# Attention over channels, then a squared-relu feed-forward: w_out combinations in one go on DVE, fold blocks in the output banks, the first group's output fourteen tiles behind

## The chip, the cores and the metric

One core of one Trainium2 chip. The metric is the device time of one execution in microseconds (us), lower is better. Engines are named as in the profile: PE (TensorE matmul), PEld (its weight loads), DVE (VectorE), ACT (ScalarE), POOL (GpSimd), SP (SyncE).

## The reference, cut to what matters

```python
# q, k, v: (4, 6080, 256) float32; w_in 256 x 2048, w_out 2048 x 256
qn = q / (norm(q, axis=1) + 1e-6);  kn = k / (norm(k, axis=1) + 1e-6)
a  = softmax(kn.T @ qn / tau)                 # 256 x 256, one for each batch
x  = (v @ a).reshape(24320, 256)
h  = x @ w_in
out = (s * relu(h)**2 + b) @ w_out
```

## The kernel before

Four ideas have to be known. (1) The attention matrix is folded into w_in: for each batch `wa = a @ w_in`, so v is multiplied by `wa` directly. (2) Tokens go in 48 groups of 512. A group has 16 *steps*, one for each tile of 128 of the 2048 hidden columns; PE does two matmuls of 512 columns a step (`mm1`), ACT a relu for each two steps. (3) All groups but the first and the last form the second product with seven instead of eight block products (`seven_items`), which needs combinations T1, T2, T3, N4 of the blocks of w_out; they are made once, during groups 0 and 1. (4) Side work is put at given steps by `at_step`, and what stands before it on an engine counts.

```python
def bank(self, name, a, b):                       # PSUM for one-off work of a batch
    if self.b == 0 and name != "wa_ps":
        return ps_o.tile(...)                     # pool of three output banks
    return ps_gram.tile(...)                      # the single Gram bank
...
def fold_one(f0, n, m):                           # a block of wa: 512 columns, one half m
    def f():
        wa_ps = self.bank("wa_ps", CH, C)...
        fold_mm(f0, n, m, wa_ps)                  # two matmuls of 512
        scaled(f0, n, m, wa_ps)                   # m == 0: evicted by ACT; m == 1: by DVE
...
def rowconst_sum(i):                              # rowconst = b * column sums of w_out
    if i < NPIECE - 1: acc = (w_pieces[0] or acc) + w_pieces[i + 1]      # DVE, 128x1024 f32
    else:              fold acc to a half                                # DVE
def rowconst_mm():
    rc_ps = ps_gram.tile(...)                     # again the Gram bank
    matmul(rc_ps, ones32, acc[:, 0, :]); rowconst = rc_ps * b            # DVE
def combine_w(i, step):                           # piece i of w_out, blocks B11 B12 B21 B22
    if step == 0:
        T1 = B12 - B11; B12 = B22 - B12           # DVE
        T3 = copy(B12)                            # ACT
    else:
        B12 = B12 + B11                           # DVE: must wait for T3's copy
        T2 = copy(B12)                            # ACT
        N4 = B21 - B12                            # DVE
...
for i, f in enumerate(fin[7:]): at_step(i // 2 * 4 + i % 2 + 1, f)       # six fold blocks
for i in range(NPIECE + 1):     at_step(14 + 2 * i, rowconst_sum(i))
at_step(26, rowconst_mm)
for i in range(NPIECE):
    for step in range(2):       at_step(24 + 2 * i + step, combine_w(i, step))
...
PLAG = {0: 12, NG - 1: 5}       # plain output of group 0 runs 12 steps behind mm1
for s in range(NS + FT):
    g, m = divmod(s, FT)
    mm1(g, m)
    ...seven-product items of group g - 1, from m == 3 on; plain output steps...
    if m % 2 == 1: relu(g, m // 2)                # ACT; frees one of two h banks
    ...squares and S sums (DVE, ACT)...
    for f in side.pop(s, []): f()
```

The Gram matmuls of batch 1 (the first product of attention, `kn.T @ qn`, in `ps_gram`) begin at step 26. An *h bank* is the PSUM memory that mm1 writes and the relu reads; there are two. S1, S2 and so on are the sums of g (the squared relu) that the seven products need. The copy that turns group 1's tokens into `vT` (eight transposes on PE, one copy on DVE) stands at step 12.

## Time and profile before

| | before |
|---|---|
| median of 3 runs, then of 4 | 747.0, then 745.96 us |
| span in the profile | 745.0 us |
| PE, DVE, ACT busy | 95%, 84%, 72% |
| PE busy between 200 and 400 us | 198.54 of 200 us |

The table says: PE bounds the kernel except at its beginning. The prediction shows the lines; in the timeline a line gives start, duration, engine, source line, operation, tiles written and read, count, and in brackets how long the engine was idle before and what ended it.

### The profile page before, as it was taken

The numbers are of one execution on the slowest core, as the hardware profiler recorded it, in microseconds if no ns is written. First come the engines' busy times: TensorE is split into PE (matmuls) and PEld (weight loads), VectorE is DVE, ScalarE is ACT, GpSimd is POOL, SyncE is SP. The second block draws the span as 40 slices with busy tenths as digits, with TensorE's granted clock in tenths as the row PEclk, the third lists the DMA queues.
The fourth block names the chain that finished last, engine by engine and source line by source line (L and its number), as shares of the span: only waits on it lengthen the run. The fifth ranks groups of instructions, "written<-read, shape, count | busy, mean of one in ns | idle before, by whom it ended". The sixth has DMA issues, their size and how long they took to land.

```text
span 745.0 us, 17832 instructions
## 1 busy us (share of the span) xinstructions
PE 711.1 (95%) x7614; PEld 511.6 (69%) x7614; DVE 626.4 (84%) x872; ACT 538.1 (72%) x573; POOL 83.7 (11%) x159
## 2 busy tenths in 40 slices
PE   4777999999999999999999999999999999999997
PEld 3534677776677777777668777777767777777776
DVE  4757799988888899989779898988888888888886
ACT  5456777777877777777777877877787777777872
POOL 5522211000102002000200111000000000000000
PEclk9999899999999999999999999999999999999999
DMA  9999959324645686432564646623332333321201
GB/s 236 209 254 133 206 116 149 70 67 102 133 90 108 123 140 119 96 91 66 110 132 114 130 98 126 136 65 72 83 71 63 72 97 73 92 61 44 79 29 73
DMA packets 83664, 80.61 MB, mean 108 GB/s; under 512 B 55712, under 2 KB 58592, under 8 KB 83584
## 3 DMA queue, kind: packets, MB, share of 16 engines
q0 software_dynamic: 23536, 40.51, 31.8%
q1 hardware_dynamic: 59616, 37.64, 19.1%
q8 instruction: 60, 0.98, 0.6%
q10 hardware_dynamic: 432, 1.31, 0.5%
q14 instruction: 20, 0.16, 0.1%
HBM read 81.00 MB, written 24.90 MB: 142 GB/s over the span
## 4 chain that ended last, share of the span: by engine, by line
PE 82%; DVE 6%; ACT 5%; DMA 4%; issue 2%; POOL 0%; DVEq 0%; ACTq 0%; POOLq 0%
PE h_ps L535 40%; PE o_ps L677 35%; PE s_ps L142 4%; ACT r L545 2%; DVE g L558 2%; DMA qk<-in_q_dram 2%; DMA qk<-in_k_dram 1%; PE wa_ps L274 1%; DMA w_in<-in_moe_w_in_dram 1%; ACT g L556 1%; DVE wa L269 1%; PE o_ps L583 1%; DVE S L603 1%; ACT wa L267 1%; DVE o_sb L563 1%
## 5 line engine op out<-in xcount | busy, mean ns | idle before, releaser
L545 ACT ACTIVATE r<-h_ps 128x1024 f16<-128x1024 f32 (+1 forms) x384 | 387.8, 1013 | 167.4 <-PE h_ps L535 165.2
L535 PE MATMUL h_ps<-vT,wa 128*128 128x512 f16 (+7 forms) x1632 | 454.6, 366 | 7.0 <-ACT r L545 5.7
L677 PEld LDWEIGHTS <-S 128*128 128x128 f16 x2944 | 198.3, 98 | 85.8 <-DVE S L603 1.0
L677 PEld LDWEIGHTS <-g 128*128 128x128 f16 x2208 | 155.9, 98 | 76.3 <-issue 2.6
L558 DVE TENSOR_TENSOR g<-r 128x2048 f16<-128x2048 f16 (+2 forms) x154 | 176.8, 1149 | 24.9 <-ACT r L545 24.8
L677 PE MATMUL o_ps<-T,S 128*128 128x128 f16 x2208 | 183.5, 219 | 1.0 <-DVE S L603 0.7
L535 PEld LDWEIGHTS <-wa 128*128 128x128 f16 x1632 | 136.6, 98 | 29.9 <-issue 7.4
L677 PE MATMUL o_ps<-w_out,g 128*128 128x128 f16 x1472 | 135.1, 220 | 0.0
L563 DVE SCALAR_TENSOR_TENSOR o_sb<-o_ps,s_out,u 128x256 f32<-128x256 f32 x138 | 66.5, 482 | 57.7 <-PE o_ps L677 54.3
L556 ACT ACTIVATE g<-r 128x1024 f16<-128x1024 f16 x92 | 96.7, 1051 | 0.0
L319 POOL DMA_DIRECT2D v<-in_v_dram x48 | 25.7, 537 | 536.1 <-DMA vT<-v 354.1
L142 PE MATMUL s_ps<-qk 128*128 128x256 f16 (+1 forms) x384 | 70.1, 283 | 15.6 <-ACT qk L133 6.8
L563 DVE SCALAR_TENSOR_TENSOR u<-o_ps,s_out,rowconst 128x256 f32<-128x256 f32 x138 | 65.9, 477 | 2.6 <-PE o_ps L677 2.6
L677 PE MATMUL o_ps<-N,g 128*128 128x128 f16 x736 | 63.4, 219 | 0.9 <-ACT nrm L222 0.9
L677 PE MATMUL o_ps<-w_out,S 128*128 128x128 f16 x736 | 63.4, 219 | 0.0
L165 ACT ACTIVATE sq<-qk 128x1024 f16<-128x1024 f16 (+3 forms) x49 | 50.5, 1034 | 11.4 <-DMA qk<-in_k_dram 7.4
L605 DVE TENSOR_TENSOR S<-S,g 128x2048 f16<-128x2048 f16 x46 | 56.3, 1224 | 1.3
L607 DVE TENSOR_TENSOR S<-g 128x2048 f16<-128x2048 f16 x46 | 55.9, 1215 | 0.0
L603 DVE TENSOR_TENSOR S<-g 128x2048 f16<-128x2048 f16 x46 | 55.9, 1215 | 0.0
L609 DVE TENSOR_TENSOR S<-g,S 128x2048 f16<-128x2048 f16 x46 | 55.9, 1214 | 0.0
L142 PEld LDWEIGHTS <-qk 128*128 128x128 f16 (+1 forms) x384 | 32.8, 101 | 21.2 <-issue 8.9
L162 DVE TENSOR_TENSOR sq<-qk 128x1024 f16<-128x1024 f16 (+3 forms) x49 | 33.0, 673 | 2.2 <-DMA qk<-in_q_dram 2.1
(67 smaller groups left out, 279.3 us busy)
## 6 DMA issues: line engine op xcount, KB each, us to landing
out_dram<-o_sb SPq DMA_DIRECT2D x46, 512.0 KB, 3.0
v<-in_v_dram POOLq DMA_DIRECT2D x47, 256.0 KB, 3.8
qk<-in_k_dram POOLq DMA_DIRECT2D x42, 256.0 KB, 6.6
qk<-in_q_dram POOLq DMA_DIRECT2D x42, 256.0 KB, 7.4
vT<-v SPq DMA_TRANSPOSE x182, 2.8
w<-in_moe_w_out_dram POOLq DMA_DIRECT2D x4, 512.0 KB, 13.6
raw<-in_q_dram ACTq DMA_DIRECT2D x2, 512.0 KB, 6.6
raw<-in_k_dram SPq DMA_DIRECT2D x2, 512.0 KB, 6.4
```

The source lines that it names most:

```text
L142: po(nc.tensor.matmul(self.s_ps[:, ch, :], kc[:np_, j, ts(ch, P)], qc[:np_, j, :], start=(c == 0 and j == 0 and ch == 0), stop=(c == len(s ...
L165: po(nc.scalar.activation(out=st["sq"][:np_, 1, js, :], in_=kc[:np_, js, :], func=AF.Square))
L535: po(nc.tensor.matmul(dst, wa[:, ci, ts(m, P)], src, start=(ci == 0), stop=(ci == CH - 1), skip_group_check=True))
L545: po(nc.scalar.activation(out=r16[:, :, i % 2, :n], in_=h_tiles.pop((g, i))[:, :, :n], func=AF.Relu))
L556: po(nc.scalar.activation(out=dst, in_=src, func=AF.Square))
L558: po(nc.vector.tensor_mul(dst, src, src))
L563: po(nc.vector.scalar_tensor_tensor(out=dst, in0=src, scalar=s_out, op0=ALU.mult, in1=add, op1=ALU.add))
L603: po(nc.vector.tensor_add(S[1], A21, A22))
L605: po(nc.vector.tensor_sub(S[2], S[1], A11))
L607: po(nc.vector.tensor_sub(S[3], A11, A21))
L609: po(nc.vector.tensor_sub(S[4], A12, S[2]))
L677: po(nc.tensor.matmul(st[name][:, j, :], a()[:, i, ts(j, P)], w[:, i, :], start=first, stop=last, skip_group_check=True))
```

## The change

The intent: DVE makes a piece's four combinations without waiting for ACT (the sum goes into B11, so B12 need not be copied first), and ACT copies them five steps later; all this starts eight steps sooner. The fold blocks rotate through three output banks, so the second no longer waits for the first one's eviction; to leave these banks free, the plain output of group 0 is put two steps later. The constant row moves from steps 14 to 26 to steps 11 to 23.

```diff
         def bank(self, name, a, b):
-            if self.b == 0 and name != "wa_ps":
+            if self.b == 0:
                 return ps_o.tile([P, a, b], FP32, tag="o_ps", name=name)
...
-    def combine_w(i, step):
+    def combine_w(i):
         part = ts(i, 2)
-        if step == 0:
-            po(nc.vector.tensor_sub(T1[:, part, :], B12, B11))
-            po(nc.vector.tensor_sub(B12, B22, B12))
-            po(nc.scalar.copy(out=T3[:, part, :], in_=B12))
-        else:
-            po(nc.vector.tensor_add(B12, B12, B11))
-            po(nc.scalar.copy(out=T2[:, part, :], in_=B12))
-            po(nc.vector.tensor_sub(N4[:, part, :], B21, B12))
+        po(nc.vector.tensor_sub(T1[:, part, :], B12, B11))
+        po(nc.vector.tensor_sub(B12, B22, B12))
+        po(nc.vector.tensor_add(B11, B11, B12))
+        po(nc.vector.tensor_sub(N4[:, part, :], B21, B11))
+
+    def cast_w(i):
+        po(nc.scalar.copy(out=T2[:, ts(i, 2), :], in_=w[:, 0, :, :P]))
+        po(nc.scalar.copy(out=T3[:, ts(i, 2), :], in_=w[:, 0, :, P:]))
...
     for i in range(NPIECE + 1):
-        at_step(14 + 2 * i, lambda i=i: rowconst_sum(i))
-    at_step(26, rowconst_mm)
+        at_step(11 + i, lambda i=i: rowconst_sum(i))
+    at_step(23, rowconst_mm)
     for i in range(NPIECE):
-        for step in range(2):
-            at_step(24 + 2 * i + step, lambda i=i, step=step: combine_w(i, step))
+        at_step(16 + 2 * i, lambda i=i: combine_w(i))
+        at_step(21 + 2 * i, lambda i=i: cast_w(i))
...
-    PLAG = {0: 12, NG - 1: 5}
+    PLAG = {0: 14, NG - 1: 5}
```

More of the change, by code (lines that the diff above doesn't have):

```diff
@@ L441, in combine_w @@
         part = ts(i, 2)
-        if step == 0:
-            po(nc.vector.tensor_sub(T1[:, part, :], B12, B11))
-            po(nc.vector.tensor_sub(B12, B22, B12))
-            po(nc.scalar.copy(out=T3[:, part, :], in_=B12))
-        else:
-            po(nc.vector.tensor_add(B12, B12, B11))
-            po(nc.scalar.copy(out=T2[:, part, :], in_=B12))
-            po(nc.vector.tensor_sub(N4[:, part, :], B21, B12))
+        po(nc.vector.tensor_sub(T1[:, part, :], B12, B11))
[3 more added lines that the diff above has]
+    def cast_w(i):
+        w = w_pieces[i].rearrange("p (i h) c -> p h i c", h=2)
+        po(nc.scalar.copy(out=T2[:, ts(i, 2), :], in_=w[:, 0, :, :P]))
+        po(nc.scalar.copy(out=T3[:, ts(i, 2), :], in_=w[:, 0, :, P:]))
     side = {}
```

## The prediction

> **What bounds the kernel now.** I read the page first (busy shares and slices), then the stretches table to see where TensorE is idle, then the timeline of 39 to 83 us, where this change acts, and the DMA issues.
>
> ```profile
> PE 711.1 (95%) x7614; PEld 511.6 (69%) x7614; DVE 626.4 (84%) x872; ACT 538.1 (72%) x573; POOL 83.7 (11%) x159
> ...
> PE   4777999999999999999999999999999999999997
> ...
> PEclk9999899999999999999999999999999999999999
> ```
>
> One slice is 18.6 us. From the fifth slice on TensorE is busy throughout, at full clock but for that slice. Slices 2 to 4 (19 to 75 us) are the only weak ones after the load. The stretches table (length, PE busy, PEld, DVE, ACT, POOL, granted clock, DMA share, GB/s) says it sharply:
>
> ```profile
> 71.00:74.00 3.00, 0.00 (x0) 0.00 (x0) 2.46 (x6) 1.28 (x3) 1.07 (x2) 1.00 1.03 115
> ...
> 76.50:78.20 1.70, 1.63 (x4) 0.55 (x4) 1.70 (x4) 1.24 (x3) 1.09 (x3) 0.50 1.05 189
> 78.20:80.00 1.80, 1.80 (x12) 1.33 (x11) 1.78 (x3) 1.53 (x2) 1.04 (x2) 0.50 1.15 206
> ...
> 81.00:82.00 1.00, 1.00 (x6) 0.44 (x5) 0.58 (x2) 0.00 (x0) 0.00 (x0) 0.50 1.15 208
> ...
> 200.00:400.00 200.00, 198.54 (x2184) 143.70 (x2184) 174.89 (x239) 152.03 (x161) 20.66 (x39) 1.00 0.53 108
> ```
>
> The steady part is bound by TensorE (198.5 of 200 us). Whatever is won before 83 us therefore reaches the end nearly whole, and nothing later can be won. One step of the program is one feed-forward tile of 128; steps 0 to 15 are group 0, and the seven-product output of group 1 begins with step 35.
>
> Three waits stand in that stretch. First, the fold blocks (a pair in each four steps, all in one bank):
>
> ```profile
> 41.77 0.68 ACT L267 ACTIVATE wa<-wa_ps,rs 128x512 f16<-128x512 f32 x1
> 41.90 0.69 DVE L558 TENSOR_TENSOR g<-r 128x1024 f16<-128x1024 f16 x1 [1.73 <-ACT r L545]
> 42.50 0.59 PE L274 MATMUL wa_ps<-w_in,eT 128*128 128x512 f16 x2 [0.83 <-ACT wa L267]
> 43.13 0.75 DVE L269 TENSOR_SCALAR wa<-wa_ps,rs 128x512 f16<-128x512 f32 x1 [0.53 <-PE wa_ps L274]
> 43.94 0.82 PE L535 MATMUL h_ps<-vT,wa 128*128 128x512 f16 x3 [0.20 <-DVE wa L269]
> ```
>
> The second block's matmuls wait for ACT to empty the bank, and the next tile waits for DVE's eviction of that block. The pattern returns at 47.89 and 51.84: a period of 3.95 us, three times.
>
> Second and third, the combinations and the constant row:
>
> ```profile
> 66.96 0.48 DVE L435 TENSOR_SCALAR rowconst<-rc_ps,b_bc 128x256 f32<-128x256 f32 x1
> 67.50 0.38 PE L142 MATMUL s_ps<-qk 128*128 128x256 f16 x2 [1.69 <-DVE rowconst L435]
> 72.72 0.40 ACT L445 CAST T<-w 128x256 f16<-128x256 f32 x1 [1.99 <-DVE w L444]
> 73.16 0.43 DVE L447 TENSOR_TENSOR w<-w 128x256 f32<-128x256 f32 x1 [0.47 <-ACT T L445]
> 74.10 0.59 PE L535 MATMUL h_ps<-vT,wa 128*128 128x512 f16 x2 [3.20 <-ACT r L545]
> 76.57 1.86 PE L535 MATMUL h_ps<-vT,wa 128*128 128x512 f16 x4 [1.23 <-ACT r L545]
> ```
>
> The Gram matmul waits 1.69 us for the bank that rowconst holds behind combinations. Then DVE and ACT wait for each other's half of a combination. A relu queued behind an ACT copy is late, TensorE is without an h bank for 3.20 and 1.23 us, and its clock falls to a half (four matmuls of 512 in 1.86 us at 76.57, against 1.02 us for four at 39.79).
>
> [...] a gap of 3.2 us, clock 0.50 from 76.5 to 82. [...] the relu at 73.03 runs only after the copy of 72.72, which itself waited 1.99 us. [...] the trace has 0.42 us for 128x256, so the combinations stay as dear as they were.
>
> **The change, part by part.**
>
> (1) Combinations. Before: 4 pieces of 4 DVE operations at 0.42 us (0.46 from start to start) and 2 ACT copies at 0.40. After: the same counts, at the same durations. Work removed: none. Removed is the return: DVE no longer waits for T3's copy before overwriting B12, because the sum goes into B11; and the copies come five steps later. They also start at step 16 instead of 24, into steps where DVE had slack (before: 8.86 busy of 13.20 us in 52 to 65.2).
>
> (2) Fold blocks in three output banks. Per pair, take 40.65 as the first block's start. Its ACT eviction is unchanged (41.77). The second block's matmuls now follow tile 2 at 41.52 instead of 42.50. DVE however takes the square first, which waits for the relu: 41.90 to 42.51. Its eviction then ends at about 43.3, so tile 4 goes on at 43.32 instead of 43.94. Gain 0.62 per pair, 1.9 us in three, not the 0.98 that TensorE's own wait suggests. Step 12 is reached at about 49.2 and its second half at 50.0 instead of 51.84.
>
> (3) The constant row is summed from step 11 instead of 14. Here a new wait comes in. The pieces of w_out are loaded by these:
>
> ```profile
> w<-in_moe_w_out_dram POOLq DMA_DIRECT2D x4, 512.0 KB, 13.6
> ```
>
> They are issued at 35.70, 36.94, 40.97 and 46.35 us; asked issue by issue, they take 14.9, 14.9, 12.3 and 8.3 us, so they land at 50.6, 51.8, 53.3 and 54.7. Before, the first sum began at 55.34, just after. Now DVE reaches it at about 50.9 and stands until 51.8, and the second until 53.3 (1.21 us each). The copy of vT for group 1 is behind the second sum: 54.5 to 55.2. Step 16 needs it, so its matmul begins at about 55.2; before it was 55.66. The fold gain shrinks to 0.46 us here.
>
> (4) Lag 14. By step 16 two output steps are done instead of four, so 2 x 0.43 us of TensorE work is pushed on to steps 28 and 29. Steps 16 to 26 go at 0.87 us each as before (2 x 0.217 for mm1, 4 x 0.11 for the output): step 26 at about 63.9 instead of 64.34. DVE meanwhile, from 55.2: two squares at 0.61, the third sum 1.15, two folds at 0.58, to about 58.85; 16 combination operations at 0.455, to 66.1; rowconst to 66.6. So the Gram matmul of step 26, ready at 64.8, still waits, to 66.65 instead of 67.50. ACT's copies find their inputs ready within 0.2 us by this reckoning.
>
> (5) Steps 27 to 35: relu, last copy, relu, Gram square, relu on ACT at 0.92, 0.80, 0.92, 0.96, 0.92; TensorE fills with output steps 28 and 29 and is held by the relu of the last tile until about 72.4. The first of the seven products begins at 73.2 instead of 78.2: 5.0 us. S1 is some 0.5 us late for the second product (it follows the last square and a Gram fold on DVE): -0.5 us. The half clock from 78.2 to 82.1, 3.9 us long, cost half of that[...]: +1.9 us.
>
> Sum: 5.0 - 0.5 + 1.9 = 6.4 us. 747.0 - 6.4 = 740.6.
>
> **Rivals.** (a) All idle time goes. From 39.8 to 78.2 TensorE has 35 steps of mm1 at 0.433 (15.2), 6 blocks (2.6), 16 output steps (6.9), transposes, rc and Gram (2.6): 27.3 of 38.4 us. With the 1.9 us of clock the ceiling is 13 us, or 734. Against it: ACT and DVE each have about 27 us of work in the same steps, and dependencies leave gaps. (b) The landing of w_out eats the whole fold gain and DVE, 3 to 4 us later than planned, is the new bound up to step 35: then only the ping-pong goes (3.2 + 1.2 us of gaps, a part of the clock), 3 to 4 us, 743.5. For it: DVE's list in (4) has no slack. (c) The gap at step 26 plus a wait for a relu behind a copy still drops the clock: 1.9 us less gain, 742.5. Against it: the folding stage before, with gaps of 0.8 us in each 4 us, ran at 1.00. (d) The gain is hidden: against it stands the 198.5 of 200 us later. (e) Slower: the Gram of batch 1 or the loads behind the copies come too late; but its first chunk needs no piece's buffer, and the copies free theirs earlier than before.
>
> **Range and chances.** The sum's weakest terms are the DVE list (about 1.5 us either way) and the clock (1.9 us). Rival (a) in part gives 737, (b) with an unlucky clock 744. The runs before scatter by 2.4 us themselves. 2% is 15 us, above even the ceiling of 13: faster 0.01, within 2% 0.98, slower 0.01.
>
> **What would show it.** In the profile after: TensorE's wait for ACT wa gone from the fold blocks, and a period near 3.3 us; DVE idle on the DMA of w before the first two sums, and TensorE waiting for vT's copy around 55; no ACT copy waiting over 0.5 us for a combination; a Gram wait of about 1.8 us on rowconst near 66; the first product near 73, at full clock. Wrong: a clock of 0.50 in 70 to 80 us, waits of 3 us for relu, a first product after 76 us, or a steady part no longer at 99%.

The sum came to 5.0 - 0.5 + 1.9 = 6.4 us, so 740.6 us. The 1.9 us are half of the 3.9 us at clock 0.50 in the profile before; that they would be won whole was the estimate.

## The result, and the profile after

The changed kernel took 739.89 us (median of 4 runs, 739.74 to 740.27), the kernel before 745.96 (4 runs, 744.75 to 747.14). The ratio is 0.992, 95% interval 0.9898 to 0.9941. Here and below a ratio is the mean time of one kernel's fast runs over that of the other's fast runs of the same rounds, so not quite the ratio of the medians quoted. All runs of this case count as fast.

The page of the changed kernel, busy shares and granted clock by slice:

```profile
PE 709.0 (96%) x7614; PEld 510.3 (69%) x7614; DVE 625.7 (85%) x872; ACT 538.1 (73%) x573; POOL 83.3 (11%) x159
...
PEclk9999999999999999999999999999999999999999
```

The work is the same, with the same counts; the slice of lower clock is gone. The stretches table of the changed kernel:

```profile
71.00:74.00 3.00, 2.63 (x21) 1.47 (x19) 2.33 (x4) 2.80 (x4) 0.89 (x2) 1.00 1.12 185
...
78.00:83.00 5.00, 5.00 (x55) 3.54 (x54) 4.67 (x7) 3.33 (x4) 0.00 (x0) 1.00 1.13 206
...
200.00:400.00 200.00, 198.53 (x2207) 144.78 (x2204) 175.16 (x240) 150.62 (x158) 22.26 (x42) 1.00 0.51 107
```

Between 71 and 74 us, where PE stood still before, it is busy for 2.63 of 3 us; between 78 and 83 us the clock is 1.00, where it was 0.50 up to 82; and the steady part is as before. The timeline of the changed kernel, at the places that the prediction named:

```profile
43.56 0.82 PE L536 MATMUL h_ps<-vT,wa 128*128 128x512 f16 x3 [0.42 <-DVE wa L269]
44.22 0.59 PE L274 MATMUL wa_ps<-w_in,eT 128*128 128x512 f16 x2
...
47.55 0.59 PE L274 MATMUL wa_ps<-w_in,eT 128*128 128x512 f16 x2
...
52.90 1.23 DVE L427 TENSOR_TENSOR acc<-w,w 128x1024 f32<-128x1024 f32 x1 [1.68 <-DMA w<-in_moe_w_out_dram]
55.41 0.68 DVE L332 COPY vT<-vT_ps 128x1024 f16<-128x1024 f16 x1
56.15 0.59 PE L536 MATMUL h_ps<-vT,wa 128*128 128x512 f16 x2 [1.55 <-DVE vT L332]
...
66.26 0.48 DVE L435 TENSOR_SCALAR rowconst<-rc_ps,b_bc 128x256 f32<-128x256 f32 x1
66.79 0.38 PE L142 MATMUL s_ps<-qk 128*128 128x256 f16 x2 [0.50 <-DVE rowconst L435]
...
73.39 0.55 PE L678 MATMUL o_ps<-w_out,g 128*128 128x128 f16 x7
```

Two fold pairs begin 3.33 us apart (44.22 and 47.55) and ACT is no longer in the bracket. DVE waits 1.68 us for a piece of w_out, and PE 1.55 us for the copy of vT that stands behind it on DVE. The first of the seven products is at 73.39 us, 4.8 us sooner than the 78.2 of before, and at full clock. (The first tile of group 0 starts 0.24 us later in this trace, at 40.03 instead of 39.79 us, before anything that was changed.) What is won reaches the end: the sum S4 of group 1 starts at 81.45 us, in the kernel before at 88.10 (second fence):

```profile
81.45 1.22 DVE L610 TENSOR_TENSOR S<-g,S 128x2048 f16<-128x2048 f16 x1
```

```profile
88.10 1.21 DVE L609 TENSOR_TENSOR S<-g,S 128x2048 f16<-128x2048 f16 x1
```

That is 6.65 us, all but 0.15 of the 6.8 us between the two spans. The chain of waits of the changed kernel (start, duration, what) says what paces it from 54 to 67 us:

```profile
41.04 13.13 DMA w<-in_moe_w_out_dram
...
54.27 1.23 DVE acc L427
```

In the stretch 48 to 80 us it runs from the landing of the third piece of w_out through DVE's list to rowconst, and only then on to PE.

### The profile page after: what moved, and what is told of

Read it like the earlier page. It is cut to its first block, busy times and chain, and to the rows that moved or that the text cites. A ratio compares the mean times of both kernels' runs of the same rounds, so it can differ in the third digit from the quotient of the medians.

```text
span 738.2 us, 17834 instructions
## 1 busy us (share of the span) xinstructions
PE 709.0 (96%) x7614; PEld 510.3 (69%) x7614; DVE 625.7 (85%) x872; ACT 538.1 (73%) x573; POOL 83.3 (11%) x159
## 4 chain that ended last, share of the span: by engine, by line
PE 80%; DVE 7%; DMA 6%; ACT 4%; issue 1%; POOL 1%; DVEq 0%; POOLq 0%
PE h_ps L536 39%; PE o_ps L678 36%; PE s_ps L142 4%; ACT r L546 2%; DMA qk<-in_q_dram 2%; DMA w<-in_moe_w_out_dram 2%; DVE g L559 2%; DMA w_in<-in_moe_w_in_dram 1%; DMA qk<-in_k_dram 1%; PE wa_ps L274 1%; DVE S L604 1%; ACT g L557 1%; PE o_ps L584 1%; DVE wa L269 1%; ACT L222 1%
## 5 line engine op out<-in xcount | busy, mean ns | idle before, releaser
L142 PE MATMUL s_ps<-qk 128*128 128x256 f16 (+1 forms) x384 | 70.3, 284 | 14.2 <-ACT qk L133 7.1
```

The costliest lines, as they stand in the source:

```text
L142: po(nc.tensor.matmul(self.s_ps[:, ch, :], kc[:np_, j, ts(ch, P)], qc[:np_, j, :], start=(c == 0 and j == 0 and ch == 0), stop=(c == len(s ...
```

## The experiments

Twelve runs, each with 4 to 6 timed executions, four kernels to a chip. The kernels built on the one before scatter by some 2 us, b_filler apart (why is the first question below); those built on the changed one by 0.2 to 1.6 us (most under 1), so their medians are compared, also where two ran on different chips. Times in us:

| run | what | median | ratio to before |
|---|---|---|---|
| (the changed kernel) | | 739.89 | 0.9920 |
| b_again | before, unchanged | 745.39 | 1.0003 |
| b_filler | before + idle matmuls in the gaps | 744.84 | 0.9989 |
| b_folds | before + fold blocks in the output banks | 743.87 | 0.9976 |
| b_form | before + one-go combination, old place | 744.31 | 0.9978 |
| b_form5 | the same, copies five steps later | 743.08 | 0.9972 |
| a_oldform | changed, old combination at the new place | 742.07 | 0.9953 |
| a_onebank | changed, fold blocks in one bank | 740.50 | 0.9931 |
| a_lag12 | changed, output twelve tiles behind | 738.72 | 0.9906 |
| a_sums13 | changed, row sums from step 13 | 739.28 | 0.9917 |
| a_rc22 | the same, rowconst matmul at step 22 | 737.79 | 0.9894 |
| a_best | the same, output twelve tiles behind | 738.02 | 0.9897 |
| a_best_fold0 | the same, fold blocks at steps 0, 4, 8 | 737.00 | 0.9883 |

My theory: waits among ACT, DVE and PE before 78 us are 4.5 us of the gain and the half clock 1.9. The rivals: the clock explains most (or none); the landing of w_out swallows the fold gain; DVE's list is the new bound.

### What the half clock costs: b_again and b_filler

b_again is the kernel before, unchanged. b_filler adds work without use, and no wait is changed:

```diff
+    def filler(n):
+        t = ps_o.tile([P, 2, C], FP32, tag="o_ps", name="fill_ps").rearrange("p a c -> p (a c)")
+        for _ in range(n):
+            po(nc.tensor.matmul(t, w_in16[:, 0, :P], w_in16[:, 0, :NW], start=True, stop=True, ...))
+    at_step(31, lambda: filler(12))
+    at_step(33, lambda: filler(4))
```

> The kernel before with 16 idle matmuls of 512 columns put into TensorE's two gaps (12 after step 31, 4 after step 33); no wait is changed. It prices the clock alone. Theory: the array stays at full clock, the four matmuls at 76.6 take 1.0 instead of 1.9 us and the products after 78 us are not at half rate: 2 to 3 us less than before. Rival, the half clock is hidden behind DVE's S sums or comes anyway: under 0.5 us.

> The kernel before, unchanged, for a second profile. So far its runs with a mean granted clock of 0.998 took 744.7 to 745.0 us and those with 0.994 to 0.996 took 745.5 to 747.4. Theory: this is one kernel with two fates of the clock after its 3.2 us gap, decided from run to run; a run of 0.998 or more shows TensorE at full clock at 76 to 82 us, with its gaps unchanged, and is up to 2.2 us shorter than one of 0.995. Rival: the times fall into two groups for another reason (loads), and the clock only goes along: then a short run shows other starts before 40 us or other waits after 83 us.

b_filler held the clock at 1.00 in its profile (0.998 to 1.000 in its six runs), and still gained only 0.8 us on the mean (0.9989, interval 0.9976 to 1.0002, so not clear of noise): my 2 to 3 us were missed. The reason is in the single times. Over three jobs and b_again I have 37 runs of the unchanged kernel with their mean clock: 17 with 0.998 took 744.6 to 745.06 us (mean 744.87); 20 with 0.994 to 0.996 took 745.5 to 747.4 (mean 746.29). b_filler's six are all within 744.57 and 745.22. b_again's profile fell on a short execution (744.84 us); its stretches:

```profile
74.00:76.50 2.50, 2.14 (x6) 0.84 (x6) 1.64 (x5) 2.50 (x5) 1.60 (x3) 0.52 1.12 298
76.50:78.20 1.70, 1.52 (x9) 0.64 (x8) 1.70 (x3) 1.49 (x3) 0.84 (x2) 0.71 1.10 200
78.20:82.00 3.80, 3.65 (x40) 2.55 (x38) 3.77 (x6) 3.79 (x5) 1.29 (x3) 1.00 1.15 184
```

The first gap is the same (PE waits 3.20 us for the relu, as in the first profile), but the half clock came at 74 instead of 76 us and was over by 78. So my expectation of a full clock in a short run was wrong as well: it is half in both, at different times. In b_again it fell on the matmuls between the two gaps, which end in a wait for a relu anyway, and that second wait shrank from 1.23 us to 0.18:

```profile
76.83 1.34 PE L535 MATMUL h_ps<-vT,wa 128*128 128x512 f16 x4 [0.18 <-ACT r L545]
```

In the execution that I predicted from it lay on the products up to 82, where PE has no wait to absorb it. Even with the full clock of b_filler PE has to wait for S1: its last product before it ends at 79.89 us, DVE's sum only at 80.31, no sooner than b_again starts on it (80.30); the execution of the prediction does so at 82.07. From the next tile on (80.81 and 82.80 us) the two traces are 2.0 us apart, as their times are (744.84 and 746.77). So the rival of b_again, that the groups have another cause, fell for these two; of the other runs only the mean clock is known, which parts them into the same two groups. The half clock costs from about nothing to 2.2 us, by where it falls; 0.8 us in the mean of the 37 runs (745.64) over the 17 short ones. The changed kernel has no such gap: clock 0.998 to 1.000 and times within 0.53 us.

### The fold blocks alone, and undone: b_folds and a_onebank

```diff
# b_folds: on the kernel before                # a_onebank: on the changed one, the reverse
-            if self.b == 0 and name != "wa_ps":
+            if self.b == 0:
```

> The kernel before with the fold blocks in the output banks alone. My theory: each of the three pairs is about 0.6 us shorter (period 3.3 instead of 3.95 us), the first constant-row sum is still late enough (about 53.5 us) not to wait for w_out, and the rest moves up whole: 1.9 us less than before (ratio about 0.9975). Rival, the landing of w_out takes it back: 0.5 us or less. The half clock at 76 to 82 us stays in both.

> The changed kernel with its fold blocks back in the single bank. My prediction held that the landing of w_out swallows most of the fold gain (0.46 of 1.9 us left at step 16). If so, undoing it costs 0 to 0.6 us (about 740.0 to 740.5): the period of the fold stage is 3.95 us again, but the wait for vT at step 16 shrinks by as much. Rival, the gains add up: 1.8 us more, as the fold blocks alone gained on the kernel before (741.7).

Alone, the fold blocks gain 0.9976, that is 1.8 us (interval 0.7 to 2.9), as expected (1.9). The trace is sharper: the first row sum starts at 53.69 us instead of 55.34 although the first tile starts 0.25 us later, so 1.9 us are won by then. Undone in the changed kernel they cost only 0.6 us (740.50 against 739.89; the expectation was 0 to 0.6, the rival 1.8). The views of waits of a_onebank (engine and line, what it waited for, us in total, times, longest) and its timeline:

```profile
PE wa_ps L274 <- ACT wa L267: 2.5, 3, 0.8
```

```profile
53.41 1.22 DVE L427 TENSOR_TENSOR acc<-w,w 128x1024 f32<-128x1024 f32 x1
...
55.81 0.68 DVE L332 COPY vT<-vT_ps 128x1024 f16<-128x1024 f16 x1
```

PE waits for ACT in the fold stage again, but DVE reaches its first sum when w_out has already landed (no bracket), and vT is copied at 55.81, 0.4 us after the changed kernel's 55.41. What the fold blocks win, the landing takes back, all but these 0.4 us.

### The combination: form, delay and place (b_form, b_form5, a_oldform)

```diff
# b_form: new combine_w and cast_w in the kernel before, old steps    # b_form5
+    at_step(24 + 2 * i, combine_w(i)); at_step(25 + 2 * i, cast_w(i))   # cast_w at 29 + 2 * i
# a_oldform: old combine_w in the changed kernel, new steps
+    at_step(16 + 2 * i + step, combine_w(i, step))
```

> The kernel before with the combinations in one go (sum into B11, copies one step later), at their old steps 24 to 30, nothing else changed. Theory: DVE's waits for T copies go, TensorE's gaps of 3.2 and 1.2 us shrink to below 1 us in all and the clock stays full: 4 to 5 us less than before. Rival, these waits only hide a plain shortage of ACT and DVE time in steps 26 to 34: gaps of over 2 us stay and the gain is under 2 us.

> The one-go combination at its old steps, as in the run that gained only 1.6 us, but with the ACT copies five steps later (29 to 35) instead of one. Theory: what held the relu was an ACT copy that waits for DVE, not DVE's wait for ACT; five steps later no copy waits, the gap of 3.3 us shrinks to under 1.5 us and the time is 3 to 5 us below before. Rival: DVE's list at steps 24 to 34 is too long at that place (evictions and squares stand in it), and relus wait for other causes: 1 to 2 us, as with one step.

> The changed kernel with the old two-step combination (sum into B12, copies at once), at its new steps 16 to 23. Theory: DVE waits for ACT in each piece (0.5 to 1 us each), its list ends 2 to 3 us later, rowconst with it, and the Gram matmul of step 26 waits 2 to 3 us instead of 0.50: 1.5 to 2.5 us more than the changed kernel. Rival: the place is all that counts, ACT has time at steps 16 to 23: within 0.5 us of the changed kernel.

b_form gained 0.9978 (1.6 us): my 4 to 5 were missed, and its rival held. The gap stays (the profile fell on its longest run, 745.48 us with a clock of 0.995):

```profile
72.74 0.40 ACT L449 CAST T<-w 128x256 f16<-128x256 f32 x1 [1.95 <-DVE w L444]
...
75.37 1.87 PE L536 MATMUL h_ps<-vT,wa 128*128 128x512 f16 x4 [3.29 <-ACT r L546]
```

DVE no longer waits for ACT, but ACT's copy waits for DVE, whose list at these steps also holds two evictions and a square; the relu behind the copy is late all the same. b_form5 delays the copies: 0.9972, 2.1 us, below my 3 to 5, and not clear of b_form (intervals 0.9960 to 0.9985 and 0.9962 to 0.9994). Its timeline and stretches, from a run of 744.47 us (three of its five runs took 742.84 to 743.08, with a clock of 0.999):

```profile
73.22 1.02 PE L536 MATMUL h_ps<-vT,wa 128*128 128x512 f16 x4 [1.23 <-ACT r L546]
...
76.63 0.28 PE L678 MATMUL o_ps<-w_out,g 128*128 128x128 f16 x2 [1.02 <-DVE g L559]
...
78.37 0.71 PE L678 MATMUL o_ps<-T,S 128*128 128x128 f16 x5 [0.91 <-DVE S L604]
```

```profile
75.00:78.40 3.40, 1.47 (x14) 0.77 (x13) 3.37 (x5) 3.40 (x6) 2.55 (x6) 1.00 1.16 197
...
78.40:81.70 3.30, 3.30 (x18) 2.11 (x19) 3.03 (x4) 2.17 (x3) 1.27 (x3) 0.50 1.15 207
```

The relu gap is 1.23 us, but DVE is so far behind that PE then waits for a square and for S1, 1.02 and 0.91 us, and the clock falls in this execution after all. a_oldform is the other half: the old form at the new place costs 742.07, 2.2 us more than the changed kernel, as expected in size, but at another place than I said:

```profile
59.54 0.40 ACT L445 CAST T<-w 128x256 f16<-128x256 f32 x1 [4.29 <-DVE w L444]
...
60.92 0.59 PE L535 MATMUL h_ps<-vT,wa 128*128 128x512 f16 x2 [1.92 <-ACT r L545]
```

Not DVE's return wait (0.4 to 0.8 us a piece) and the Gram matmul behind rowconst, but a relu behind an ACT copy that has come to its turn 4.29 us before DVE, whose list still holds row sums and squares, has made its input. Between 39.8 and 83 us PE waits for a relu five times, 4.2 us in all, where the changed kernel has two such waits, 1.5 us in all. (DVE waited for w_out for only 0.88 us here, less than in the changed kernel, so the landing is not what makes it late.) A pair that I did not plan prices the place: b_form5 and a_onebank have the same form, delay and fold bank and differ only in the place of these works, the constant row with them, and in the lag; 743.08 against 740.50, 2.6 us. So the useful part is the delay of the copies and the earlier place together; writing the sum into B11 is what permits the delay. How much of a_oldform's 2.2 us is the form and how much the delay is not shown: the new form at the new place with the copies at once was not run.

### The landing of w_out and DVE's list: a_sums13 and a_rc22

```diff
# a_sums13, on the changed kernel
-        at_step(11 + i, lambda i=i: rowconst_sum(i))
+        at_step(13 + i, lambda i=i: rowconst_sum(i))
# a_rc22: that, and
-    at_step(23, rowconst_mm)
+    at_step(22, rowconst_mm)
```

> The changed kernel with the constant-row sums from step 13 instead of 11, so that the copy of vT and one square pass DVE before it waits for w_out. Theory (landing of w_out is what holds DVE and, through vT, TensorE at 54.6 to 56.1): the 1.55 us wait for vT goes, DVE's list ends about 1.3 us sooner, 1.0 to 1.5 us less than the changed kernel (about 738.6). Rival, the wait is only moved to the h banks, since ACT or DVE bounds steps 16 to 35 anyway: within 0.3 us of the changed kernel.

> The changed kernel with the sums from step 13 and the constant row's matmul at step 22, so that its eviction stands on DVE before the last combination. With the sums from 13 alone the Gram matmul waited 2.04 us for rowconst at 66.1. Theory: that wait falls to under 0.4 us and 1.0 to 1.5 us of it reach the end: 737.8 to 738.3. Rival: DVE's squares and S sums behind it bound steps 27 to 37, and it moves to a wait for S or a relu: 739.0 to 739.3 as with the sums alone.

With the sums from step 13 the copy of vT passes ahead of them, and DVE no longer waits for w_out; PE's wait for vT falls from 1.55 to 0.35 us. The time fell by 0.6 us only (739.28; expected 1.0 to 1.5). The rest turned into this wait, the first line below; the other two are a_rc22:

```profile
66.11 0.38 PE L142 MATMUL s_ps<-qk 128*128 128x256 f16 x2 [2.04 <-DVE rowconst L435]
```

```profile
64.30 0.38 PE L142 MATMUL s_ps<-qk 128*128 128x256 f16 x2
...
70.90 0.55 PE L678 MATMUL o_ps<-w_out,g 128*128 128x128 f16 x7
```

PE arrives at the Gram matmul of step 26 sooner and finds the bank held until DVE's list has come to rowconst: the rival in my expectation named h banks, but the kind is right, a moved wait. One step sooner for rowconst puts its eviction (at 63.58 us) ahead of the last combination; the wait is gone, though PE now waits 0.42 us for the last row sum; the first product is at 70.90 us and the time 737.79, at the lower edge of the expected 737.8 to 738.3.

### The lag, and a version that beats both (a_lag12, a_best, a_best_fold0)

```diff
# a_lag12, on the changed kernel; a_best: on a_rc22
-    PLAG = {0: 14, NG - 1: 5}
+    PLAG = {0: 12, NG - 1: 5}
# a_best_fold0: on a_best
-        at_step(i // 2 * 4 + i % 2 + 1, f)
+        at_step(i // 2 * 4, f)
```

> The changed kernel with the first group's output twelve instead of fourteen tiles behind. Theory: two output steps (0.87 us of TensorE) run in the wait for the relu at 51.6 to 52.7 us instead of in steps 28 and 29, where TensorE and ACT are near each other; 0.3 to 0.9 us less. Rival: the two output steps of 28 and 29 fill a stretch that ACT bounds, so moving them only opens a gap: no change; or the output banks collide with fold blocks at step 12: slower.

> The one before with the output twelve tiles behind as well. The lag alone gained 1.2 us, in waits for relu and vT that are smaller here, so 0.3 to 0.9 us of it should remain: 737.2 to 737.8. Rival: without these waits the two output steps cost at steps 12 and 13 what they save at 28 and 29: within 0.2 us of the one before.

> The one before with each pair of fold blocks one step (two for the second) sooner, at steps 0, 4 and 8, so that their evictions stand ahead of the relu and the square on ACT and DVE. Theory: the period of the fold stage falls from 3.3 to about 3.0 us or less, 1 us by step 12; w_out lands when it does, so DVE waits for it again and 0.2 to 0.8 us remain: 736.6 to 737.4. Rival: the landing takes all of it: no change. Rival: the relu behind an eviction holds the h banks longer: slower.

Twelve instead of fourteen gained 1.2 us on the changed kernel (738.72), more than the 0.3 to 0.9 expected: the output banks are free in time, since the last fold block is evicted by step 11 (at 49.34 us, 0.74 us long; the first output step begins at 50.37 without a wait), and two output steps run while PE would wait for a relu and for vT (these waits fall from 1.11 and 1.55 us to 0.67 each). In its profile the landing too was a little sooner (first sum at 52.26 instead of 52.90), so not all of the 1.2 need be the lag. On a_rc22, where those waits are gone, twelve gains nothing (738.02 against 737.79, and the runs overlap: 737.94 to 738.13 and 737.60 to 738.03): the rival. The two seem to be ways to the same microsecond.

Fold blocks at steps 0, 4 and 8, ahead of relu and square, shorten the pair to 3.00 us; in the timeline of a_best_fold0:

```profile
43.22 0.59 PE L536 MATMUL h_ps<-vT,wa 128*128 128x512 f16 x2 [0.25 <-ACT r L546]
...
46.22 0.59 PE L536 MATMUL h_ps<-vT,wa 128*128 128x512 f16 x2 [0.25 <-ACT r L546]
```

It gains 1.0 us on a_best and is the fastest of all: 737.00 us, ratio 0.9883 (0.9870 to 0.9897), 2.9 us less than the changed kernel, with correct output. It was not tried with fourteen tiles.

## Why the prediction was right, point by point

**The time and its class** were right: 739.89 against 740.6, within 737.0 to 744.0, and within 2% as it gave 0.98 to. The two terms of its sum were mis-sized against each other, the waits too small by 0.5 us and the clock too large by 0.8: that the sum comes within 0.7 us of the measured time is in part luck.

**The steady part** hands the gain on whole: shown by 6.65 us at S4 against 6.8 in the span.

**Step (1), combinations.** Right that no work goes and that a relu behind a copy is what PE waits for. a_oldform shows that the new form with its delay is worth 2.2 us at the new place. Not right in weight: the text put the return wait first and the five steps of delay after it; b_form removes the return (and copies one step later), and a gap of 3.29 us stays. Delay and place count, and the form permits the delay.

**Step (2), fold blocks.** Right: period 3.33 us in the trace, and 1.9 us won by the first row sum in b_folds; that its time fell by 1.8 us, so near to 1.9, is luck within an interval of 0.7 to 2.9.

**Step (3), the landing.** Right in kind, and the most useful step. Mis-sized: the first two pieces took 15.7 and 15.8 us instead of 14.9 (landing at 51.5 and 52.8), the first sum began at 52.90 instead of 51.8, and step 16 at 56.15 instead of 55.2. That is 0.5 us later than before the change, 0.24 of it from the later start of the trace, so of the fold gain nothing was left there instead of 0.46 us. a_onebank confirms it independently (0.6 us).

**Step (4), DVE's list.** The end of rowconst was put at 66.6 and is at 66.74. The Gram matmul waited 0.50 instead of 1.85 us because PE itself came 1.5 us late, at 66.29 instead of 64.8: one microsecond from step 16, and some 0.4 from the rowconst matmul, which the change moves ahead of step 26 and which the working left out of these steps. a_sums13, without the delay at step 16, shows 2.04. Together they confirm the part of rival (b) that calls DVE's list the pace of this stretch; its 743.5 us did not come, since it supposed this list 3 to 4 us later than planned, and it ended 0.1 us later.

**Step (5).** First product at 73.39 instead of 73.2. The 0.5 us for a late S1 did not come: PE goes over to S1 at 75.53 without a gap. (Rival (a) gave ACT and DVE about 27 us of work each between 39.8 and 78.2 us; the trace has 24.1 and 25.6.)

**The clock** is the term of the sum that failed in size. The prediction took 1.9 us from one profile and started from 747.0, both of an execution with the half clock on the products. On the mean of 37 runs it is 0.8 us. The waits won more than the 4.5 predicted: 744.87 (the 17 short runs) to 739.89 is 5.0 us. In the rounds of the result the gain was 6.07 by medians: 5.0 of waits and 1.1 of clock, against 4.5 and 1.9. Rival (c), that a smaller gap still drops the clock, did not come for the changed kernel (1.00 from 70 to 82 us); in b_form5 it did, with a clock of 0.50 from 78.40 to 81.70 us after PE's waits of 1.23, 1.02 and 0.91 us. So that the half clock would go with the gap of 3.20 us was not a safe estimate.

**Left open:** why the pieces of w_out take some 1.5 us more in one kernel than in another that issues them at nearly the same times (the first, issued at 35.76 us in the changed kernel and at 35.97 in a_sums13, took 15.7 and 14.2 us), and how much of a_lag12's gain is such an earlier landing rather than the lag.

## What to carry to other kernels

When a two-engine ping-pong is on the path, look at what is queued behind each half: here the loss was not DVE's wait for ACT but the relu behind ACT's copy. Cutting the return alone left the gap at 3.29 us, giving the copy room brought it to 1.23, and only with the earlier place as well did most of the time come back. Before work is moved earlier, read when its data lands: here DVE's wait of 1.68 us for w_out held the copy of vT behind it, and PE waited 1.55 us for that copy, 0.35 when it passed first (a_sums13). So let what PE needs pass first. And look at single times with their clock before a term is taken from one profile: with the same gap of 3.2 us the same kernel took 744.8 us in one profile and 746.8 in another.
